# Folding the query weights with the feature map as stationary operand, in sixteen 32x32 tiles, with a turn by DMA

## Chip, cores and metric

One core of one Trainium2 chip. The time is that of one execution on the device in microseconds, as the median of several; the kernel before takes 271.53 us (three runs, 271.49 to 271.55). An engine's instructions run in the order in which they stand; between engines semaphores hold an instruction back until what it needs is there. TensorE is PE, VectorE DVE, ScalarE ACT, GpSimd POOL; SP is the engine that only issues DMAs, in one queue.

## What is computed

For x of 2048 tokens by 1024 columns, a gated mix of linear attention (a) and an expert of one token (b), in bfloat16:

```python
q, k, v = heads(x @ wqkv)                       # 32 heads of 32 columns
pq, pk = q @ w_phi[h], k @ w_phi[h]             # per head, 32 x 32
phi = concat(softmax(p), softmax(-p))           # 64 features a head
kv, z = phi_k.T @ v, phi_k.sum(tokens)
a = (phi_q @ kv / (phi_q @ z + 1e-6)) @ wo
r = x @ w_r; idx = argmax(r)                    # one token
y = (silu(x[idx] @ w_gate) * (x[idx] @ w_up)) @ w_down * sigmoid(r[idx])
out = g * a + (1 - g) * (x + y at row idx)      # g = sigmoid(x @ gate_w)
```

## The kernel before

Tokens go in 16 tiles of 128, the transposed x (`xT`) stays in SBUF. The feature map is folded into the projections ahead of use: `wkf = Wk · w_phi`, `wqf = Wq · w_phi` (eight row blocks `kb` of 128 each, so 16 folds), and pk, pq are then single products of `xT` with them.

Stage one (to 70 us) makes the values `v_all` (`k_v`, three pieces of 256, 384 and 386 columns a tile; the last carries two extra columns, the routing score and the gate, copied to `rg` by DVE) and the folds. `wT_load` brings one block of Wk or Wq transposed, 0.25 MB by a transposing DMA on the SP queue, into one of six slots of the two buffers `shv`; `fold` makes 8 matmuls of 128 columns with that block as stationary operand and the block-diagonal feature map `BDm` as moving one, and DVE copies the two results out. `FOLDS` says how many folds follow a tile. At the end `route` finds the token of the expert: scores are turned on PE, DVE takes the best of each tile, SP sends it to one partition (`mrow`), DVE takes the best of all (`mxv` ... `ixi`), SP reads `ixi` into a register and loads that row of x (`rows`), and PE and ACT turn it into `xs` (`xs_turn`).

Stage two (70 to 140 us) has 32 units of key features, a half tile each: `feats` is 8 matmuls into one of two PSUM buffers `pk`, two exponentials on ACT into `e` (four buffers), the sums `ssum` and reciprocals `rs` on DVE, `ksum` and the product `phi` on POOL (every fourth `phi` on DVE). Five units later `k_kv` adds phi-by-value into `kvps` (three PSUM banks, cleared by DVE after the first two value tiles). Between them stand the expert's products: `ffn_gu` for r = 0 to 3 (`facc`, 32 or 16 matmuls with 32 stationary columns at four column places), each over three or four buffers `wch` of 1 MB. These come from three pools: A the ring of three, D the two `shv` buffers once the folds are through, W and V the halves of `wob`. A string such as "AAAD" names the buffers of one product in order. `gate_load` holds the first three back until the last block of Wq has landed.

Stage three (140 us on) has the query units: `pq` as above, `phi` turned by DMA (`phT`), `num` = phi_q by `KV`, the division on DVE into `o_sb`, its turn by DMA (`oT`), `po` by `wo`, the mix on DVE and the store. `kv_finish` copies `kvps` to `KV`, two copies on DVE and two on ACT.

The order in which the engines' instructions stand is set by a scheduler that takes the program of these loops and may move an instruction ahead of others on its engine; it is fixed before the run. DMAs on SP wait in order, too.

Of the kernel before, what the change touches and what calls it, by code (L numbers as in the profile page):

```python
# [18 lines left out]
P = 128  # L19
# [18 lines left out]
TX = 4  # L38
FOLDS = [0] * 8 + [1, 2, 2, 2, 2, 2, 2, 3]
TDV = 0  # L40


def general_path(tc, A_wqkv, A_w_phi, A_wo, x2, out2, gate, omg, y2, idx_pool, xT, wqf, ident, BDm):
# [31 lines left out]
    for kb in range(KB):  # L75
        nc.sync.dma_start_transpose(out=wkT[:, :, kb * P:(kb + 1) * P], in_=A_wqkv[kb * P:(kb + 1) * P, D:2 * D])
        for jh in range(2):
            for j4 in range(4):
                j = jh * 4 + j4
                nc.tensor.matmul(pp[:].rearrange("p h f -> p (h f)")[:, j4 * P:(j4 + 1) * P],  # L80
                                 lhsT=wkT[:, j, kb * P:(kb + 1) * P], rhs=BDm[:, j, :], start=True, stop=True)
            nc.vector.tensor_copy(out=wkf[:, kb, jh * 512:(jh + 1) * 512], in_=pp[:].rearrange("p h f -> p (h f)"))
    nc.vector.memset(kvp[:], 0.0)
# [6 lines left out]
    def features(w):  # L90
        for hf in range(2):
            for kb in range(KB):
                nc.tensor.matmul(pp[:].rearrange("p h f -> p (h f)"), lhsT=xTt[:, kb, :],
                                 rhs=w[:, kb, hf * 512:(hf + 1) * 512], start=(kb == 0), stop=(kb == KB - 1))
            nc.vector.tensor_reduce(out=mm[:, 0, :], in_=pp[:], axis=AX.X, op=ALU.max)
            nc.vector.tensor_reduce(out=mm[:, 1, :], in_=pp[:], axis=AX.X, op=ALU.min)
            for s in range(2):
                nc.vector.tensor_tensor(out=sh[:, s], in0=pp[:], in1=_bc(mm[:, s, :], [P, HH, DH]), op=ALU.subtract)
                nc.scalar.activation(out=sh[:, s], in_=sh[:, s], func=ACTF.Exp, scale=(1.0 if s == 0 else -1.0))
            nc.vector.tensor_reduce(out=sr[:], in_=sh[:], axis=AX.X, op=ALU.add)  # L100
            nc.vector.reciprocal(out=sr[:], in_=sr[:])
            for s in range(2):
                nc.vector.tensor_tensor(out=phi[:, hf * HH:(hf + 1) * HH, s, :], in0=sh[:, s],
                                        in1=_bc(sr[:, s, :], [P, HH, DH]), op=ALU.mult)

    with tc.For_i(0, S, P) as r0:
        nc.vector.tensor_copy(out=xTt[:], in_=xT[:, :, bass.ds(r0, P)])
        for hf in range(2):
# [3 lines left out]
            nc.scalar.copy(out=va[:, hf * HH:(hf + 1) * HH, 0:DH], in_=pv[:])  # L112
        features(wkf)
        for pr in range(HH):
            nc.tensor.matmul(slot(kvp, pr), lhsT=phi[:, 2 * pr:2 * pr + 2].rearrange("p h s f -> p (h s f)"),
                             rhs=va[:, 2 * pr:2 * pr + 2, :].rearrange("p h d -> p (h d)"),
                             start=False, stop=False, skip_group_check=True)
    for pr in range(HH):
        nc.vector.tensor_copy(out=KVp[0:64, pr, 0:33], in_=slot(kvp, pr)[0:64, 0:33])
        nc.vector.tensor_copy(out=KVp[64:128, pr, 33:66], in_=slot(kvp, pr)[64:128, 33:66])  # L120

    with tc.For_i(0, NT, 1) as t:
# [3 lines left out]
        nc.vector.tensor_copy(out=gt[:, 1:2], in_=omg[:, bass.ds(t, 1)])  # L126
        features(wqf)
        for g in range(2):
# [18 lines left out]
        for nh in range(2):  # L147
            sl = slice(nh * 512, (nh + 1) * 512)
            for kb in range(KB):
# [15 lines left out]
def kernel(  # L165
# [130 lines left out]
    def wT_load(which, kb):  # L296
        n = (which * KB + kb) % 6
        wT[which, kb] = shv[n // 4][:, n % 4, :].rearrange("p (k f) -> p k f", f=P)
# [247 lines left out]
    def v_out(t, c, pv):  # L546
# [3 lines left out]
        if c == 2:  # L550
            nc.vector.tensor_copy(out=rg[:, :, t], in_=pv[:, D - lo:VW - lo])

    def v_first():
# [13 lines left out]
        for t in (1, 0):  # L567
            for c in range(3):
# [4 lines left out]
                v_out(t, c, acc[t, c])  # L573
        nc.vector.memset(kvps[:], 0.0)
        nc.vector.memset(kvps[:, 0:16 * KSTR].rearrange("p (r c) -> p r c", c=KSTR)[:, :, DH:66:DH + 1], 5e-7)

    kst = {}

    def feats(u, wf, is_q):
# [3 lines left out]
        for kb in range(KB):  # L583
            nc.tensor.matmul(pkf, lhsT=xT[:, kb, t * P:(t + 1) * P], rhs=wf[:, kb, hf * 512:(hf + 1) * 512],  # L584
                             start=(kb == 0), stop=(kb == KB - 1))
# [39 lines left out]
    def kv_finish():  # L625
        kvr = kvps[:, 0:HH * KSTR].rearrange("p (r c) -> p r c", c=KSTR)
        for hf in range(2):
            for h2 in range(2):
                (nc.vector.tensor_copy, nc.scalar.copy)[hf](out=KV[hf][h2 * 64:h2 * 64 + 64, :, h2 * 33:h2 * 33 + 33],
                                      in_=kvr[h2 * 64:h2 * 64 + 64, hf * NPU:(hf + 1) * NPU, h2 * 33:h2 * 33 + 33])  # L630
# [81 lines left out]
    def wload(n):  # L712
        wn["want"] += n
        while wq and wn["done"] < min(wn["want"], wn["folded"] + 6):
            wT_load(*wq.pop(0))
# [17 lines left out]
    for t in range(TX, NT):  # L733
# [3 lines left out]
        for n, c in enumerate((2, 0, 1) if t == NT - 1 else (0, 1, 2)):  # L737
            k_v(t, c)
            if c == 2 and t == NT - 1:
                route()  # L740
            if n >= 3 - FOLDS[t]:
                w, kb = fq.pop(0)
                fold(w, wkf if w == 0 else wqf, kb)
                wn["folded"] += 1
                wload(1 if t + TX >= NT else 0)
    LAG = 5
# [10 lines left out]
    while i < 2 * NU or n_next < NU or wos:  # L757
        if i in GU:
            r = GU.index(i)
            ffn_gu(r, ("AAAD", "DWVA", "AADD")[r])  # L760
            if r == 2:
                ffn_gu(3, "WV")
        if i == DN - 3:
# [125 lines left out]
```

## Time and profile before

| | |
|---|---|
| median of 3 runs | 271.53 us (271.49 to 271.55) |
| the profiled execution | 271.29 us |
| its span, first to last instruction | 269.7 us |
| PE busy | 262.6 us, 97% |
| DVE, POOL, ACT busy | 73%, 47%, 44% |
| clock granted to PE | full in all 40 slices |
| DMA | 56.35 MB, 209 GB/s on average |

The profile's busy time counts instructions, and matmuls overlap, so 97% says that PE nearly always has one, not that it works at its peak. The chain that ended last is followed back from the last instruction to what released each; where it lies on an engine without holes, that engine's work sets the time there, and time taken off it is time off the kernel until another engine's work becomes the later one. Row prefixes such as L584 are lines of the kernel.

### The profile page before, as it was taken

The numbers are of one execution on the slowest core, as the hardware profiler recorded it, in microseconds if no ns is written. First come the engines' busy times: TensorE is split into PE (matmuls) and PEld (weight loads), VectorE is DVE, ScalarE is ACT, GpSimd is POOL, SyncE is SP. The second block draws the span as 40 slices with busy tenths as digits, with TensorE's granted clock in tenths as the row PEclk, the third lists the DMA queues.
The fourth block names the chain that finished last, engine by engine and source line by source line (L and its number), as shares of the span: only waits on it lengthen the run. The fifth ranks groups of instructions, "written<-read, shape, count | busy, mean of one in ns | idle before, by whom it ended". The sixth has DMA issues, their size and how long they took to land.

```text
span 269.7 us, 5421 instructions
## 1 busy us (share of the span) xinstructions
PE 262.6 (97%) x2023; PEld 143.5 (53%) x2023; DVE 195.8 (73%) x344; ACT 119.0 (44%) x229; POOL 128.0 (47%) x113
## 2 busy tenths in 40 slices
PE   7999999999999999999999999999999999999993
PEld 3666667777544455545554444454444454454442
DVE  3020025556889896999998999879889797888772
ACT  3153332332355555545556565546455435534110
POOL 6000000000086989739789998554554535554110
PEclk9999999999999999999999999999999999999999
DMA  7999999997950699759936699899998899999642
GB/s 237 239 161 194 177 190 314 159 184 203 412 202 0 190 413 391 260 196 345 389 86 235 138 205 209 172 202 213 237 172 170 176 226 153 200 169 205 153 117 67
DMA packets 102522, 56.35 MB, mean 209 GB/s; under 512 B 85132, under 2 KB 90332, under 8 KB 102492
## 3 DMA queue, kind: packets, MB, share of 16 engines
q1 hardware_dynamic: 99692, 51.29, 76.9%
q10 hardware_dynamic: 2768, 4.67, 7.0%
q8 instruction: 17, 0.28, 0.4%
q14 instruction: 13, 0.11, 0.1%
q0 software_dynamic: 32, 0.00, 0.0%
HBM read 31.27 MB, written 4.20 MB: 132 GB/s over the span
## 4 chain that ended last, share of the span: by engine, by line
PE 89%; DVE 4%; DMA 2%; ACT 1%; issue 1%; ACTq 0%; POOL 0%
PE po L693 20%; PE pk L584 20%; PE pv L542 18%; PE pq L584 17%; PE num L654 3%; PE kvps L620 3%; PE pW L307 3%; PE facc L478 2%; DVE ssum L592 2%; PE pv L564 1%; DMA shv<-in_A_x_dram 1%; DMA oT<-o_sb 1%; PE kvps L564 1%; DVE rq L599 1%; PE small_ps L496 1%
## 5 line engine op out<-in xcount | busy, mean ns | idle before, releaser
L592 DVE TENSOR_REDUCE ssum<-e 128x32 f32<-128x1024 bf16 x64 | 76.9, 1203 | 6.8 <-ACT e L588 6.6
L605 POOL TENSOR_TENSOR phi<-e,rq 128x1024 bf16<-128x1024 bf16 x32 | 60.9, 1912 | 40.7 <-DVE rq L599 32.7
L584 PEld LDWEIGHTS <-xT 128*128 128x128 bf16 x512 | 47.4, 98 | 52.5 <-issue 1.3
L693 PE MATMUL po<-wo_sb,oT 128*128 128x512 bf16 (+2 forms) x264 | 60.0, 372 | 0.5 <-DMA oT<-o_sb 0.5
L584 PE MATMUL pq<-wqf,xT 128*128 128x512 bf16 x256 | 60.3, 379 | 0.0
L584 PE MATMUL pk<-wkf,xT 128*128 128x512 bf16 x256 | 59.9, 379 | 0.0
L542 PE MATMUL pv<-wv_sb,xT 128*128 128x256 bf16 (+2 forms) x336 | 52.1, 307 | 0.0
L605 POOL TENSOR_TENSOR phi<-e,rs 128x1024 bf16<-128x1024 bf16 x25 | 47.8, 1912 | 2.3 <-DVE rs L599 1.2
L542 PEld LDWEIGHTS <-xT 128*128 128x128 bf16 x336 | 31.7, 97 | 14.5
L549 ACT CAST v_all<-pv 128x384 bf16<-128x384 f32 (+1 forms) x45 | 20.1, 447 | 41.5 <-PE pv L542 35.7
L587 ACT ACTIVATE e<-pq 128x512 bf16<-128x512 f32 x32 | 19.0, 594 | 40.4 <-PE pq L584 37.8
L693 PEld LDWEIGHTS <-oT 128*128 128x128 bf16 x264 | 23.8, 98 | 23.7 <-DMA oT<-o_sb 0.6
L587 ACT ACTIVATE e<-pk 128x512 bf16<-128x512 f32 x32 | 19.1, 597 | 29.2 <-PE pk L584 21.4
L420 POOL COPY wch<-shv 1x1 bf16<-1x1 bf16 x3 | 0.4, 178 | 57.2 <-DMA shv<-in_A_wqkv_dram 57.2
L697 DVE SCALAR_TENSOR_TENSOR oo<-po,gate,xg 128x512 bf16<-128x512 f32 (+2 forms) x33 | 24.0, 727 | 4.3 <-PE po L693 4.2
L602 POOL TENSOR_TENSOR ksum<-ksum,ssum 128x32 f32<-128x32 f32 x32 | 14.0, 438 | 22.4 <-DVE ssum L592 20.8
L659 DVE TENSOR_TENSOR o_sb<-num,rden 128x512 bf16<-128x512 f32 x32 | 21.7, 677 | 0.8
L588 ACT ACTIVATE e<-pq 128x512 bf16<-128x512 f32 x32 | 18.9, 591 | 0.0
L588 ACT ACTIVATE e<-pk 128x512 bf16<-128x512 f32 x32 | 18.9, 591 | 0.0
L678 ACT ACTIVATE xg<-xin,omg 128x1024 f32<-128x1024 bf16 x16 | 18.3, 1148 | 0.5
L309 DVE CAST wkf<-pW 128x512 bf16<-128x512 f32 x16 | 10.6, 686 | 9.5 <-PE pW L307 9.5
L654 PEld LDWEIGHTS <-phT 128*128 128x128 bf16 x256 | 12.4, 98 | 8.0 <-issue 0.7
(133 smaller groups left out, 199.8 us busy)
## 6 DMA issues: line engine op xcount, KB each, us to landing
wch<-in_B_w_down_dram SPq DMA_DIRECT2D x7, 1024.0 KB
wch<-in_B_w_up_dram SPq DMA_DIRECT2D x6, 1024.0 KB
wch<-in_B_w_gate_dram SPq DMA_DIRECT2D x4, 1024.0 KB
xin<-in_A_x_dram ACTq DMA_DIRECT2D x16, 256.0 KB
out_dram<-oo SPq DMA_DIRECT2D x30, 128.0 KB
wch<-in_B_w_gate_dram SPq DMA_DIRECT2D x4, 768.0 KB
wv_sb<-in_A_wqkv_dram SPq DMA_DIRECT2D x8, 256.0 KB
wo_sb<-in_A_wo_dram SPq DMA_DIRECT2D x1, 2048.0 KB
```

Source lines behind the costliest of these rows:

```text
L542: nc.tensor.matmul(pv[:, 0:hi - lo], lhsT=xT[:, kb, t * P:(t + 1) * P], rhs=wv_sb[:, kb, lo:hi], start=(kb == 0), stop=(kb == KB - 1))
L549: nc.scalar.copy(out=v_all[:, t, h0:h1, 0:DH], in_=pv[:, 0:(h1 - h0) * DH].rearrange("p (h d) -> p h d", d=DH))
L584: nc.tensor.matmul(pkf, lhsT=xT[:, kb, t * P:(t + 1) * P], rhs=wf[:, kb, hf * 512:(hf + 1) * 512], start=(kb == 0), stop=(kb == KB - 1))
L587: nc.scalar.activation(out=e[:, :, 0, :], in_=pk[:], func=ACTF.Exp)
L588: nc.scalar.activation(out=e[:, :, 1, :], in_=pk[:], func=ACTF.Exp, scale=-1.0)
L592: nc.vector.tensor_reduce(out=ssum[:], in_=e2, axis=AX.X, op=ALU.add)
L605: eng.tensor_tensor(out=phi[:].rearrange("p h s f -> p (h s) f"), in0=e2, in1=_bc(rs, [P, HH * 2, DH]), op=ALU.mult)
L654: nc.tensor.matmul(num[:, pl * 66:pl * 66 + 66], lhsT=phT[:, pl, :], rhs=KV[hf][:, pl, :], start=True, stop=True)
L659: nc.vector.tensor_tensor(out=st["o"][:, hf * HH:(hf + 1) * HH, :].rearrange("p (r h) d -> p r h d", h=2), in0=nv[:, :, :, 0:DH], in1=rden ...
L678: nc.scalar.activation(out=xg, in_=st["xin"][:], func=ACTF.Copy, scale=omg[:, t:t + 1])
L693: nc.tensor.matmul(po[:, 0:w], lhsT=st["oT"][:, kb, :], rhs=moe["wo"][:, kb, sl], start=(kb == 0), stop=(kb == KB - 1))
L697: nc.vector.scalar_tensor_tensor(out=o_out[:, 0:w], in0=po[:, 0:w], scalar=gate[:, t:t + 1], in1=st["xg"][:, sl], op0=ALU.mult, op1=ALU.add)
```

## The change

The key folds move to tiles 5 to 12, one each. The query blocks are all loaded (eight slots now), and folded in four packs, after pieces of tiles 13, 14 and 15. A pack has `BDm`'s 32x32 blocks as stationary operands at all sixteen places of the array and 512 columns of the loaded blocks as moving ones. Its four results lie in the three banks of `kvps` and one other; DVE and ACT copy two each to `wfT` (two buffers of the ring A), and eight transposing DMAs turn `wfT` into `wqf`, whose columns stand in another order, which `q_heads` undoes where pq reads them. `kvps` is cleared later, by ACT (`kv_zero`). The copies of `rg` go to ACT, the last two copies of `kv_finish` to DVE; `route` comes one piece earlier. The buffers of the expert's products are taken in another order. (The general path, a branch for other data, has small edits and is not run.)

```diff
-FOLDS = [0] * 8 + [1, 2, 2, 2, 2, 2, 2, 3]
+FOLDS = [0] * 5 + [1] * 8 + [0] * 3
+PACKS = {(13, 2): (0, 0), (14, 1): (1, 0), (15, 0): (0, 1), (15, 2): (1, 1)}
...
+def q_heads(wqf, kb, hf):
+    return wqf[:, kb, hf * 512:(hf + 1) * 512].rearrange("p (r c f) -> p c r f", r=4, f=DH)
...
     def wT_load(which, kb):
-        n = (which * KB + kb) % 6
+        n = kb
...
+    def qfold(a, half):
+        if (a, half) == (0, 0):
+            moe["wfT"] = [ring.tile([P, 4, D], BF, name="wfT", tag="wch") for _ in range(2)]
+        pB = psB.tile([P, 512], F32, name="pW", tag="pB")
+        banks = [kvps[:, 0:512], kvps[:, 512:1024], kvps[:, 1024:1536], pB[:]]
+        for r in range(4):
+            for c in range(4):
+                j = 4 * a + c
+                nc.tensor.matmul(banks[r][32 * c:32 * c + 32, :].rearrange("p (k d) -> p k d", d=P),
+                                 lhsT=BDm[32 * r:32 * r + 32, j, 32 * r:32 * r + 32],
+                                 rhs=shv[half][32 * r:32 * r + 32, :, j * P:(j + 1) * P],
+                                 start=True, stop=True, tile_position=(32 * r, 32 * c), skip_group_check=True)
+        for r in range(4):
+            (nc.vector.tensor_copy, nc.scalar.copy)[r % 2](out=moe["wfT"][a][:, r, half * 512:(half + 1) * 512], in_=banks[r])
+
+    def qfold_turn():
+        for ar in range(8):
+            nc.sync.dma_start_transpose(out=wqf[:, :, ar * P:(ar + 1) * P], in_=moe["wfT"][ar // 4][:, ar % 4, :])
+
+    def kv_zero():
+        one = ones[:, 0:1]
+        nc.scalar.activation(out=kvps[:], in_=one.to_broadcast([P, 3 * 512]), func=ACTF.Copy, scale=0.0)
+        nc.scalar.activation(out=kvps[:, 0:16 * KSTR].rearrange("p (r c) -> p r c", c=KSTR)[:, :, DH:66:DH + 1],
+                             in_=one.unsqueeze(2).to_broadcast([P, 16, 2]), func=ACTF.Copy, scale=5e-7)
...
         if c == 2:
-            nc.vector.tensor_copy(out=rg[:, :, t], in_=pv[:, D - lo:VW - lo])
+            nc.scalar.copy(out=rg[:, :, t], in_=pv[:, D - lo:VW - lo])
...
-        nc.vector.memset(kvps[:], 0.0)
-        nc.vector.memset(kvps[:, 0:16 * KSTR].rearrange("p (r c) -> p r c", c=KSTR)[:, :, DH:66:DH + 1], 5e-7)
...
-            nc.tensor.matmul(pkf, lhsT=xT[:, kb, t * P:(t + 1) * P], rhs=wf[:, kb, hf * 512:(hf + 1) * 512],
+            nc.tensor.matmul(pk[:].rearrange("p (c r) f -> p c r f", r=4) if is_q else pkf,
+                             lhsT=xT[:, kb, t * P:(t + 1) * P],
+                             rhs=q_heads(wf, kb, hf) if is_q else wf[:, kb, hf * 512:(hf + 1) * 512],
...
-                (nc.vector.tensor_copy, nc.scalar.copy)[hf](out=KV[hf][h2 * 64:h2 * 64 + 64, :, h2 * 33:h2 * 33 + 33],
+                (nc.vector.tensor_copy, nc.scalar.copy)[0](out=KV[hf][h2 * 64:h2 * 64 + 64, :, h2 * 33:h2 * 33 + 33],
...
-        while wq and wn["done"] < min(wn["want"], wn["folded"] + 6):
+        while wq and wn["done"] < min(wn["want"], wn["folded"] + 8):
...
-            if c == 2 and t == NT - 1:
+            if n == 1 and t == NT - 1:
                 route()
...
-                wload(1 if t + TX >= NT else 0)
+                wload(4 if t + TX >= NT else 0)
+            if (t, n) in PACKS:
+                qfold(*PACKS[t, n])
+    qfold_turn()
...
-            ffn_gu(r, ("AAAD", "DWVA", "AADD")[r])
+            ffn_gu(r, ("WVDD", "AAAW", "VDDA")[r])
             if r == 2:
-                ffn_gu(3, "WV")
+                ffn_gu(3, "AA")
...
         if i == 2:
+            kv_zero()
             gates()
```

On DVE, at the end of stage one and the start of stage two (mi, mrow, mxv, cnd, ixf, ixi, hl are the routing's small tiles; wfT and wqf the folded query weights; e, ssum, rs those of a key unit). Before:

```order
L331 TENSOR_TENSOR mi<-mi,row_144 16x1
L315 RECIPROCAL gate<-eg 128x16
L316 TENSOR_SCALAR omg<-gate 128x16
L592 TENSOR_REDUCE ssum<-e 128x32
L599 RECIPROCAL rs<-ssum 128x32
L592 TENSOR_REDUCE ssum<-e 128x32
L335 TENSOR_REDUCE mxv<-mrow 1x1
L599 RECIPROCAL rs<-ssum 128x32
L337 TENSOR_SCALAR cnd<-mrow,mxv 1x16
L339 TENSOR_TENSOR cnd<-cnd,mrow 1x16
L592 TENSOR_REDUCE ssum<-e 128x32
L341 TENSOR_REDUCE ixf<-cnd 1x1
```

and now:

```order
L361 TENSOR_TENSOR mi<-mi,row_144 16x1
L329 CAST wfT<-kvps 128x512 x2
L365 TENSOR_REDUCE mxv<-mrow 1x1
L367 TENSOR_SCALAR cnd<-mrow,mxv 1x16
L369 TENSOR_TENSOR cnd<-cnd,mrow 1x16
L371 TENSOR_REDUCE ixf<-cnd 1x1
L373 CAST ixi<-ixf 1x1
L390 TENSOR_SCALAR hl<-ixi 1x1
L622 TENSOR_REDUCE ssum<-e 128x32
L629 RECIPROCAL rs<-ssum 128x32
L622 TENSOR_REDUCE ssum<-e 128x32
L629 RECIPROCAL rs<-ssum 128x32
```

mxv, which reads what the DMA of mrow brought, stood behind the second sum, and the instructions from cnd to hl among later sums; all six now stand ahead of the first sum.

On the SP queue, same place (wch are the expert's buffers, gate and up its weights; shv the loaded blocks; rows the expert's token). Before:

```order
L299 DMA_TRANSPOSE shv<-in_A_wqkv_dram 128x8x128 x10
L454 DMA wch<-in_B_w_gate_dram 128x2x2048 x4
L333 DMA mrow<-mi 1x16x2
L454 DMA wch<-in_B_w_gate_dram 128x2x1536
L454 DMA wch<-in_B_w_up_dram 128x2x512
L344 TENSOR_LOAD ixi
L344 ISA x2
L345 ISA
L345 DMA rows<-in_A_x_dram 8x128
```

and now:

```order
L304 DMA_TRANSPOSE shv<-in_A_wqkv_dram 128x8x128 x8
L484 DMA wch<-in_B_w_gate_dram 128x2x2048 x3
L484 DMA wch<-in_B_w_gate_dram 128x2x1536
L333 DMA_TRANSPOSE wqf<-wfT 128x8x128
L363 DMA mrow<-mi 1x16x2
L333 DMA_TRANSPOSE wqf<-wfT 128x8x128 x3
L374 TENSOR_LOAD ixi
L374 ISA x2
L375 ISA
L375 DMA rows<-in_A_x_dram 8x128
L333 DMA_TRANSPOSE wqf<-wfT 128x8x128 x4
L484 DMA wch<-in_B_w_gate_dram 128x2x2048
```

One turn of the query weights (wqf<-wfT) stands ahead of mrow, three behind it, and the last four behind the load of rows and ahead of the fourth buffer (128x2x2048) of the first product.

On ACT, at the start of stage two. Before:

```order
L549 CAST v_all<-pv 128x8x32
L549 CAST v_all<-pv 128x12x32
L587 ACTIVATE e<-pk 128x16x32
L588 ACTIVATE e<-pk 128x16x32
L587 ACTIVATE e<-pk 128x16x32
L588 ACTIVATE e<-pk 128x16x32
```

and now:

```order
L579 CAST v_all<-pv 128x8x32
L579 CAST v_all<-pv 128x12x32
L329 CAST wfT<-pW 128x512
L329 CAST wfT<-kvps 128x512
L617 ACTIVATE e<-pk 128x16x32
L618 ACTIVATE e<-pk 128x16x32
L337 ACTIVATE kvps<-const-bfloat16-1.0 128x1536
L617 ACTIVATE e<-pk 128x16x32
L618 ACTIVATE e<-pk 128x16x32
L338 ACTIVATE kvps<-const-bfloat16-1.0 128x16x2
```

The copies of the last pack stand ahead of the first exponentials, and the clearing of kvps between the first pair and the second.

## Rows read from the trace of the kernel before

**Rows 1.** Page, part 1: busy time, share of the span, instructions
```profile
PE 262.6 (97%) x2023; PEld 143.5 (53%) x2023; DVE 195.8 (73%) x344; ACT 119.0 (44%) x229; POOL 128.0 (47%) x113
```

**Rows 2.** Chain that ended last, 13 to 90 us: start us, us, what
```profile
38.46 0.45 PE pW L307 x8
38.91 2.17 PE pv L542 x16
...
41.53 1.31 PE pv L542 x8
...
70.15 8.63 PE pk L584 x40
```

**Rows 3.** Busy time by stage (us, engine busy, instructions, PEclk, DMA share, GB/s)
```profile
13.20:70.15 56.95, 56.95 (x484) 40.09 (x481) 23.59 (x57) 20.54 (x48) 0.41 (x3) 1.00 0.97 207
```

**Rows 4.** The same chain ahead of the first expert product
```profile
83.00 0.94 PE pk L584 x5
...
84.81 0.60 ACT e L587
...
86.22 1.91 PE facc L478 x32
```

**Rows 5.** The chain at the turn to the queries
```profile
146.69 1.13 DVE ssum L592
...
148.19 1.09 DVE ssum L592
...
157.93 0.42 PE num L654 x8
```

**Rows 6.** Timeline there: start, us, instruction [idle before, releaser]
```profile
151.89 0.38 ACT L629 CAST KV<-kvps 64x264 bf16<-64x264 f32 x1 [2.43 <-DVE KV L629]
...
153.79 1.22 DVE L592 TENSOR_REDUCE ssum<-e 128x32 f32<-128x1024 bf16 x1 [0.30 <-ACT e L588]
```

**Rows 7.** The chain around the second expert product
```profile
96.80 0.25 PE kvps L620 x8
...
98.91 1.84 PE facc L478 x32
100.75 0.36 PE kvps L620 x8
```

**Rows 8.** Groups by form: busy us, mean ns, idle before
```profile
L678 ACT ACTIVATE xg<-xin,omg 128x1024 f32<-128x1024 bf16 x16 | 18.3, 1148 | 0.5
...
L483 ACT COPY gs<-facc 128x512 f32<-128x512 f32 x4 | 2.3, 586 | 3.8 <-PE facc L478 3.8
```

**Rows 9.** Timeline of ACT, first key features
```profile
73.64 0.60 ACT L587 ACTIVATE e<-pk 128x512 bf16<-128x512 f32 x1 [0.64 <-PE pk L584]
```

**Rows 10.** Timeline of the SP queue, 59 to 82 us
```profile
59.05 1.23 SPq L299 DMA_TRANSPOSE shv<-in_A_wqkv_dram  x1
62.77 2.33 SPq L454 DMA_DIRECT2D wch<-in_B_w_gate_dram  x4
71.45 0.65 SPq L333 DMA_DIRECT2D mrow<-mi  x1
...
80.35 0.38 SPq L345 DMA_DIRECT2D rows<-in_A_x_dram  x1
```

**Rows 11.** Timeline of DVE, same stretch
```profile
73.03 1.22 DVE L592 TENSOR_REDUCE ssum<-e 128x32 f32<-128x1024 bf16 x1 [1.23 <-ACT e L588]
...
76.68 0.16 DVE L335 TENSOR_REDUCE mxv<-mrow 1x1 f32<-1x16 f32 x1 [0.70 <-DMA mrow<-mi]
...
78.78 0.08 DVE L343 CAST ixi<-ixf 1x1 uint32<-1x1 f32 x1
```

**Rows 12.** Timeline of GpSimd, same stretch
```profile
74.78 1.91 POOL L605 TENSOR_TENSOR phi<-e,rs 128x1024 bf16<-128x1024 bf16 x1
...
77.24 1.91 POOL L605 TENSOR_TENSOR phi<-e,rs 128x1024 bf16<-128x1024 bf16 x1 [0.34 <-DVE cnd L337]
...
79.32 1.91 POOL L605 TENSOR_TENSOR phi<-e,rs 128x1024 bf16<-128x1024 bf16 x1
```

More of the change, by code (lines that the diff above doesn't have):

```diff
@@ L81, in general_path @@
                                  lhsT=wkT[:, j, kb * P:(kb + 1) * P], rhs=BDm[:, j, :], start=True, stop=True)
-            nc.vector.tensor_copy(out=wkf[:, kb, jh * 512:(jh + 1) * 512], in_=pp[:].rearrange("p h f -> p (h f)"))
+            nc.scalar.copy(out=wkf[:, kb, jh * 512:(jh + 1) * 512], in_=pp[:].rearrange("p h f -> p (h f)"))
     nc.vector.memset(kvp[:], 0.0)
@@ L92, in features @@
             for kb in range(KB):
-                nc.tensor.matmul(pp[:].rearrange("p h f -> p (h f)"), lhsT=xTt[:, kb, :],
-                                 rhs=w[:, kb, hf * 512:(hf + 1) * 512], start=(kb == 0), stop=(kb == KB - 1))
+                nc.tensor.matmul(pp[:].rearrange("p (c r) f -> p c r f", r=4), lhsT=xTt[:, kb, :],
+                                 rhs=w(kb, hf), start=(kb == 0), stop=(kb == KB - 1))
             nc.vector.tensor_reduce(out=mm[:, 0, :], in_=pp[:], axis=AX.X, op=ALU.max)
@@ L112, in general_path @@
             nc.scalar.copy(out=va[:, hf * HH:(hf + 1) * HH, 0:DH], in_=pv[:])
-        features(wkf)
+        features(lambda kb, hf: wkf[:, kb, hf * 512:(hf + 1) * 512].rearrange("p (c r f) -> p c r f", r=4, f=DH))
         for pr in range(HH):
@@ L117, in general_path @@
                              start=False, stop=False, skip_group_check=True)
-    for pr in range(HH):
-        nc.vector.tensor_copy(out=KVp[0:64, pr, 0:33], in_=slot(kvp, pr)[0:64, 0:33])
-        nc.vector.tensor_copy(out=KVp[64:128, pr, 33:66], in_=slot(kvp, pr)[64:128, 33:66])
+    kvr = kvp[:, 0:HH * KSTR].rearrange("p (r c) -> p r c", c=KSTR)
+    nc.vector.tensor_copy(out=KVp[0:64, :, 0:33], in_=kvr[0:64, :, 0:33])
+    nc.vector.tensor_copy(out=KVp[64:128, :, 33:66], in_=kvr[64:128, :, 33:66])
     with tc.For_i(0, NT, 1) as t:
@@ L126, in general_path @@
         nc.vector.tensor_copy(out=gt[:, 1:2], in_=omg[:, bass.ds(t, 1)])
-        features(wqf)
+        features(lambda kb, hf: q_heads(wqf, kb, hf))
         for g in range(2):
```

## Prediction

> **What bounds the kernel now.** I read the page first, then the chain that ended last in order of time, then the timelines of the places that the change touches. The page shows TensorE (PE) busy for 97% of the span [rows 1]. The chain shows the first stage, values and weight folds, as PE work without a hole until 70.15 us, at granted clock 1.00 [rows 2, 3]; the key features (pk) follow. The little that is lost stands at known places: PE waits some 0.3 us for ScalarE (ACT) ahead of the first expert product at 86.22 [rows 4], and a little at 157.93, where num follows a chain on VectorE (DVE) [rows 5]. So there are two questions: what the change takes off PE, and which other engine, off the chain by about a microsecond, takes its place.
>
> **PE, the folds.** Sixteen folds of eight matmuls stand in the chain with 0.45 us each [rows 2]. The eight of the key weights stay, four tiles earlier; the eight of the query weights go: 8 x 0.45 = 3.6 us off a stage that is PE alone. In their place come four packs of sixteen 32x32 matmuls of 512 columns. A full matmul of 512 columns takes a slot of 8.63 / 40 = 0.216 us [rows 2]. The nearest row to a pack is the expert product, whose matmuls use 32 columns of the array each: 32 of them take 1.84 us, 8 slots and 0.11 [rows 7]. So four on different columns cost one slot; the next 66-column group takes 0.36 us instead of 0.25 [rows 7], so going in and out of the narrow form is 0.2 us together. No row shows tiles on different rows of the array. If all sixteen overlap, a pack is 0.22 + 0.2 = 0.42 us; if only the columns overlap, 4 x 0.22 + 0.2 = 1.08. I take 0.52, near the lower end, since the columns overlap fully: 4 x 0.52 = 2.1 us, within 1.7 to 4.3. The last pack also needs bank 2 cleared by DVE, which has the gate and routing instructions between its copies now: I add 0.3. Net -3.6 + 2.1 + 0.3 = -1.2, and pk starts at 68.95 instead of 70.15.
>
> The Trainium skill ("TensorE: Matmul & The Clock Gate", Part 3: Packing small matmuls) gives 660 ns for sixteen 32x32 tiles of 512 columns. By it the packs are 4 x 0.66 = 2.64 us and PE gains 0.5 us less. No run here shows it yet.
>
> **DVE and ACT in the first stage.** Of the sixteen copies of query weights eight go to ACT, and so do the rg copies. PE waited for neither engine there, so I cost it at nothing; the cover is that each is busy for less than half of the stage [rows 3].
>
> **ACT, the clearing of kvps.** It moves from DVE (first stage, hidden) to ACT, behind the first pair of exponentials. No row shows ACT clearing 1536 columns; 512 columns take 0.59 us and 1024 take 1.15 [rows 8], so 1.7 us by the same step. A pair of exponentials takes 1.1 us and ACT idles 0.64 to the next [rows 9]. With 1.7 us between, the second pair ends some 0.65 us after the fourth pk wants its buffer (there are two): PE waits 0.65 us. Bounds: 0 if it is half as long, 1.0 if it is a quarter longer.
>
> **DVE, the new wait.** This decides. Today the routing result mrow goes out at 71.45 and has landed at 76.68, when mxv reads it; DVE has done its first sums (ssum) by then [rows 10, 11]. In the changed order DVE has mxv ahead of its first ssum. So the first sum starts when mrow lands (M) plus the chain down to hl, six small instructions of 0.08 to 0.16 us: M + 0.9.
>
> When is M? Today mrow stands behind four loads of 1 MB, issued from 62.77: 13.9 us from the first issue to mrow's landing [rows 10, 11]. The first load leaves 3.7 us after the last query block's issue at 59.05 [rows 10], since it is held until that block has landed. In the change that block waits for the last key fold. A tile is 2.17 + 1.31 = 3.48 us [rows 2], so the last key fold ends at 38.46 + 3 x 0.45 (folds of tiles 5 to 7) + 0.45 + 4 x (3.48 + 0.45) = 56.0, and the first load leaves at 59.7. Ahead of mrow are then 3.75 MB of loads and one turn of 0.25 MB. By the same 13.9 us M = 73.6. A transpose moves its quarter megabyte slower (the stage full of them has the DMA 97% busy at 207 GB/s [rows 3], the loads go at 4 MB in under 13.9 us): +0.6, M = 74.2. It cannot be before 71, as mrow leaves near 69.5; I keep 72.5 to 75.2.
>
> What follows: the pitch of a sum with its reciprocal is 1.5 us [rows 5], the first phi on GpSimd starts 1.75 after its sum's start, then one each 2.1, 1.9 long [rows 11, 12]. The third phi ends at M + 0.9 + 1.75 + 2 x 2.1 + 1.9 = M + 8.75. PE needs it for the third kvps group (0.26), and the eighth pk (1.73) follows: its end is M + 10.95 with 0.2 of latency. Today it ends at 83.00 + 1.73 = 84.73 [rows 4]. PE's own pace gives 68.95 + 0.65 + 8 x 1.73 + 3 x 0.26 = 84.2. So the shift there is max(-0.5, M - 73.8): with M = 74.2, **+0.4**. The PE gain of 1.2 us is eaten, and would be at any price of the packs below 0.8 us.
>
> **SP queue and the expert's buffers.** The eight turns are issued ahead of the fourth expert buffer, 1.3 us each (1.23 for a transpose [rows 10]). ixi is made at M + 0.85; today the row load follows it by 1.6 us (78.78 to 80.35) [rows 10, 11]; then four turns and the load, at M + 8.0. With what is left of the turns in the queue (some 1.8 us) and 1 MB per 3.5 us (13.9 / 4) it lands at M + 13.3. The product starts 1.5 us after the eighth pk (exponentials and xs) [rows 4], at M + 12.45, and needs that buffer after 24 matmuls, M + 13.85. Half a microsecond to spare: cost 0. The later expert loads have time: the second product is some 12 us behind [rows 4, 7], and the query weights are needed at 140.
>
> **DVE at the turn to the queries.** Two KV copies of 0.4 us each come over from ACT, between the sums. DVE is the chain there, from 146.69 to num at 157.93 [rows 5]: +0.8. ACT, which now stands 2.43 us for those copies, has the exponentials ready earlier, which gives back DVE's wait of 0.30 [rows 6]: net **+0.45** at num, which PE meets directly. Bounds 0 to 0.8.
>
> **Sum.** +0.4 + 0.45 = +0.85. The profiled execution took 271.29 us (span 269.7); the median 271.53 is 0.24 above. So 271.29 + 0.85 = 272.15 for an execution like that one, **272.3** as a median.
>
> **Rivals.**
> (1) PE's gain comes through: faster. If mrow lands by 73.2 or before (a start-up that the two early loads have behind them, a turn as fast as a load: M near 72.5), the shift is -0.5, or -1.2 if the clearing hides too; and with ACT free earlier the KV copies may cost nothing. Time 270.3 to 271.0, say 270.7. Against it: the 13.9 us are this very queue. For it: a third of a microsecond decides.
> (2) The fourth expert buffer is late: slower. Point: landing after M + 13.85. Each microsecond beyond is one for PE; if the turns each hold the DMA 0.4 us longer than their issue, 8 x 0.4 - 0.5 = 2.7 on PE, 275.0; at half that, 273.4. For it: all eight turns stand ahead of it in one queue.
> (3) The tiles do not overlap across rows: packs of 1.08 us, so pk starts 2.2 later and PE's own pace gives 86.4: +1.7 + 0.45, 273.7. If instead the four columns of one row group go one after another, each a slot and a weight load of 0.1, a pack is 4 x 0.32 + 0.2 = 1.5 us, PE's pace gives 88.1 and the time is 275.3. Rows 7 speak against that: there four tiles of one row group share a slot. The second form is what the same page of the Trainium skill says of weight loads (they overlap running matmuls only where the row group differs); by that rule the expert product would not have been 1.84 us, so the trace does not bear it out.
> (4) The query matmuls, which now read their 512 columns in runs of 32, lose a column per run: 256 x 16 / 2.4 GHz = 1.7 us, 274. No row shows such a read, for or against.
> That the change does not do what it says is excluded by the order: the 64 narrow matmuls and the eight turns are in it.
>
> **Chances.** The forecast's case 0.48 (within it: slower 0.28, same 0.20); rival 1 0.25 (faster 0.22, same 0.03); rival 2 0.15 (slower 0.11, same 0.04); rival 3 0.08 (slower 0.07, same 0.01; its second form 0.01 of it); rival 4 0.04, slower. A measurement tells about 0.2%, 0.54 us. Together faster 0.22, same 0.28, slower 0.50. The forecast's case alone spans 271.5 to 272.9; the range to hold 8 in 10 goes to 270.4 for most of rival 1 and to 273.8 for rival 3 and half of rival 2.
>
> **What would show it.** Right: a wait of DVE at mxv for mrow of 2 to 4 us, ended near 74; kvps waiting for phi near 80; the eighth pk ending near 85; no wait inside the first expert product; packs of half a microsecond; num at 158.8 after DVE. Wrong: mxv without a wait, pk running through from 69, packs over 0.8 us, or PE standing inside the expert product.

## The result, and the profile after

The changed kernel takes 275.37 us (the median of 274.13, 275.25, 275.49 and 701.08) against 271.51 for the kernel before on the same chip (271.41 to 271.55). The ratio is 1.0122, with a 95% interval of 1.0089 to 1.0155: slower, by some 3.3 us as this ratio has it, and outside the range that was forecast. The execution of 701.08 is left out of the ratio, as are two of a later run (e7, 280.06 and 280.33), and no profile shows what happened in them. The profiled execution took 275.49 us, its span is 273.5 us (269.7 before).

The page's busy line answers to [rows 1]. Under it stand the rows of PE's timeline that the prediction spoke of (start, length, engine, line, operation, tile and forms, count, and in brackets the wait ahead of it with what ended it).

```profile
PE 261.4 (96%) x2023; PEld 140.0 (51%) x2023; DVE 190.5 (70%) x320; ACT 124.8 (46%) x253; POOL 128.0 (47%) x113
```

```profile
59.35 0.42 PE L324 MATMUL kvps<-shv,BDm 32*32 32x512 bf16 x12
59.39 0.39 PE L324 MATMUL pW<-shv,BDm 32*32 32x512 bf16 x4
59.71 2.35 PE L572 MATMUL pv<-wv_sb,xT 128*128 128x256 bf16 x16
...
68.20 0.42 PE L324 MATMUL kvps<-shv,BDm 32*32 32x512 bf16 x12 [0.33 <-DVE wfT L329]
68.25 0.40 PE L324 MATMUL pW<-shv,BDm 32*32 32x512 bf16 x4
68.58 9.03 PE L612 MATMUL pk<-wkf,xT 128*128 128x512 bf16 x40
80.11 0.43 PE L650 MATMUL kvps<-v_all,phi 128*128 128x66 bf16 x8 [2.50 <-POOL phi L635]
...
84.53 1.89 PE L612 MATMUL pk<-wkf,xT 128*128 128x512 bf16 x8
...
87.91 1.48 PE L508 MATMUL facc<-wch,xs 128*32 128x512 bf16 x24
90.54 0.62 PE L508 MATMUL facc<-wch,xs 128*32 128x512 bf16 x8 [1.16 <-DMA wch<-in_B_w_gate_dram]
```

A pack of sixteen tiles goes from 59.35 to the next matmul at 59.71: 0.36 us. The key features start at 68.58; before they start at 69.98:

```profile
69.98 8.80 PE L584 MATMUL pk<-wkf,xT 128*128 128x512 bf16 x40
```

So PE's gain is there, 1.4 us, and two waits eat it: 2.50 us for phi, and 1.16 us inside the first expert product for its fourth buffer. Before, that product began at 86.22 and ran through [rows 4]; now it begins at 87.91.

What the first wait goes back to stands on DVE's timeline. The chain that ended last names both waits as DMA (columns: start, length, what):

```profile
75.33 0.16 DVE L365 TENSOR_REDUCE mxv<-mrow 1x1 f32<-1x16 f32 x1 [4.23 <-DMA mrow<-mi]
...
76.17 0.14 DVE L373 CAST ixi<-ixf 1x1 uint32<-1x1 f32 x1
...
76.41 1.20 DVE L622 TENSOR_REDUCE ssum<-e 128x32 f32<-128x1024 bf16 x1
```

```profile
69.18 6.12 DMA mrow<-mi
84.89 5.61 DMA wch<-in_B_w_gate_dram
```

Before, DVE's first sum stood at 73.03 and mxv behind it [rows 11]. Now the first sum stands behind mxv, and so behind mrow, at 76.41. SP's queue, with what it issues (of the first row the landings are 65.1, 68.4, 71.0 and 73.2 by the trace's DMA events):

```profile
59.66 4.04 SPq L484 DMA_DIRECT2D wch<-in_B_w_gate_dram  x4
66.84 2.19 SPq L333 DMA_TRANSPOSE wqf<-wfT  x1
69.18 0.65 SPq L363 DMA_DIRECT2D mrow<-mi  x1
69.92 5.99 SPq L333 DMA_TRANSPOSE wqf<-wfT  x3
78.08 0.40 SPq L375 DMA_DIRECT2D rows<-in_A_x_dram  x1
78.59 6.20 SPq L333 DMA_TRANSPOSE wqf<-wfT  x4
84.89 0.54 SPq L484 DMA_DIRECT2D wch<-in_B_w_gate_dram  x1
```

And the stretch of these stages as a whole, by windows (PE busy and count, granted clock, DMA share, GB/s), before and after:

```profile
59.50:101.00 41.50, 41.37 (x363) 1.00 0.67 234
```

```profile
59.50:101.00 41.50, 37.32 (x327) 18.41 (x312) 30.35 (x52) 24.04 (x49) 21.40 (x23) 1.00 0.97 279
```

(The second row has a column for each engine, PE first.) The stretch holds more DMA work than before, but 0.97 does not say that the DMA was full. The share adds up the times of the packets that began in a stretch, and over single microseconds it goes above 1 (2.19 from 71 to 72, at 237 GB/s). Shorter windows of the changed kernel show a hole: while SP waited for the index, between the fourth turn and the fifth, the DMA had next to nothing to do, and just before, with nothing but turns in it, it moved 280 GB/s.

```profile
75.00:77.00 2.00, 2.00 (x11) 1.00 1.27 280
77.00:80.00 3.00, 0.60 (x3) 1.00 0.14 27
```

Where the 3.3 us are, read off PE's timeline against before: key features start 1.4 earlier; from there to the first expert product 3.1 more (19.33 instead of 16.24); inside it 1.33; from it to the first query feature nothing; at the turn to the queries 0.3 in the end. Together 3.3, up to DVE's last instruction (268.75 against 265.43). The span grew by another 0.5 behind that; in the profiles of this study that last piece is anywhere from 3.2 to 4.75 us, so I count it as nothing.

### The profile page after: what moved, and what is told of

The parts are those of the page before. It is cut to its first block, busy times and chain, and to the rows that moved or that the text cites. A ratio compares the mean times of both kernels' runs of the same rounds, so it can differ in the third digit from the quotient of the medians.

```text
span 273.5 us, 5439 instructions
## 1 busy us (share of the span) xinstructions
PE 261.4 (96%) x2023; PEld 140.0 (51%) x2023; DVE 190.5 (70%) x320; ACT 124.8 (46%) x253; POOL 128.0 (47%) x113
## 4 chain that ended last, share of the span: by engine, by line
PE 80%; DVE 8%; DMA 7%; SPq 1%; issue 1%; ACT 0%; POOL 0%; DVEq 0%
PE po L723 20%; PE pv L572 17%; PE pq L612 16%; PE pk L612 15%; DVE ssum L622 4%; PE num L684 3%; PE kvps L650 3%; DMA mrow<-mi 2%; DMA wch<-in_B_w_gate_dram 2%; DMA wv_sb<-in_A_wqkv_dram 2%; PE facc L508 2%; PE pW L312 1%; DMA oT<-o_sb 1%; PE kvps L594 1%; PE pv L594 1%; SPq L333 1%
## 5 line engine op out<-in xcount | busy, mean ns | idle before, releaser
L572 PE MATMUL pv<-wv_sb,xT 128*128 128x256 bf16 (+2 forms) x336 | 51.1, 307 | 0.0
L650 PEld LDWEIGHTS <-phi 128*128 128x128 bf16 x256 | 11.6, 99 | 10.6 <-POOL phi L635 5.1
```

The lines of the kernel that those rows point to most:

```text
L572: nc.tensor.matmul(pv[:, 0:hi - lo], lhsT=xT[:, kb, t * P:(t + 1) * P], rhs=wv_sb[:, kb, lo:hi], start=(kb == 0), stop=(kb == KB - 1))
L650: nc.tensor.matmul(kv_slot(pr), lhsT=phi[:, 2 * pl:2 * pl + 2, :, :].rearrange("p h s f -> p (h s f)"), rhs=v_all[:, t, hf * HH + 2 * pl:h ...
```

## The experiments

My theory from these rows: two losses in a row (mrow's wait on DVE, the late fourth buffer), both from SP's order, and a small one at the KV copies. The rivals: PE's own pace, the fourth buffer alone, or the DMA as such.

### One edit each, and all three

**e1**, mrow on another queue.

```diff
-        nc.sync.dma_start(out=mrow[0:1, :, :], in_=mi[:])
+        nc.scalar.dma_start(out=mrow[0:1, :, :], in_=mi[:])
```

> The changed kernel with one edit: the small routing transfer mrow is issued from ScalarE's queue instead of SP's, so it stands behind no load and no turn. The scheduler answers by putting the fourth expert buffer on SP ahead of the row load and of the last four turns. Theory (VectorE's first key sum stands behind mxv, which waits for mrow; the fourth buffer stands behind the turns): mrow lands near 71.5 to 72 instead of 75.3, mxv waits under 1 us, the eighth pk ends at 83.3 to 84.3 instead of 86.3, no wait of PE inside the first expert product, 271.0 to 272.3 us. Rival A (PE itself is slower in the key stage: packs, clearing of kvps): the eighth pk still ends near 86, 274 to 275. Rival B (the fourth buffer alone is the loss): the eighth pk unchanged, the stall of 1.16 us gone, 274.0 to 274.3. Rival C (the 2 MB of turns slow the DMA for all that follows): mrow early, but the fourth buffer still lands near 90, so PE stands 4 us inside the product and the time stays near 275.

Measured: 275.86 us, ratio 1.0156 (1.0108 to 1.0205). mrow did not come earlier. The issue on ACT's queue, and DVE's reader:

```profile
68.82 0.61 ACTq L363 DMA_DIRECT2D mrow<-mi  x1
```

```profile
75.70 0.16 DVE L365 TENSOR_REDUCE mxv<-mrow 1x1 f32<-1x16 f32 x1 [4.43 <-DMA mrow<-mi]
```

Issued at 68.8 from a queue of its own it lands no earlier than from SP. So my theory fell in one point: it is not the queue. What the DMA engines had taken on before it came first all the same. The first product runs through here, since the scheduler had moved its fourth buffer up, but it starts at 89.57: PE had waited 2.94 us for phi, and its clock stood at the half level (1.2 GHz) from 81 to 83 (0.50).

**e2**, half the turns behind the fourth buffer (`qfold_turn(0, 4)` where it was, `qfold_turn(4, 8)` behind `ffn_gu(0)`).

> The changed kernel with one edit: the last four of the eight turns are issued after the fourth expert buffer instead of ahead of it; mrow stays where it is in SP's queue. Theory (mrow's wait and the late fourth buffer are two separate losses): mrow lands near 75.3 as before, the eighth pk ends at 86.0 to 86.5, the stall of 1.16 us inside the first expert product goes, 273.9 to 274.4 us. Rival B (the fourth buffer is all of the loss beyond the KV copies): 271.8 to 272.5. Rival C (the DMA is short of bandwidth, whatever the order): the stall stays within 0.3 us, 275.

Measured: 274.67 us, 1.0107 (1.0067 to 1.0146). The product runs through (first row), but it starts at 89.20 and not at 87.9, and the windows show why: the clock fell to its half level after PE's wait of 2.67 us, and part of the pk behind it ran at that.

```profile
80.10 0.62 PE L650 MATMUL kvps<-v_all,phi 128*128 128x66 bf16 x8 [2.67 <-POOL phi L635]
83.58 0.41 PE L650 MATMUL kvps<-v_all,phi 128*128 128x66 bf16 x8
...
89.20 1.91 PE L508 MATMUL facc<-wch,xs 128*32 128x512 bf16 x32
```

```profile
78.00:82.00 4.00, 1.90 (x12) 0.73 0.55 145
82.00:86.00 4.00, 4.00 (x30) 0.85 1.24 211
```

From one kvps group to the next it is 3.48 us here and 2.08 in the changed kernel (80.11 to 82.19, clock 1.00). So the 1.3 us of the buffer were won, and lost again to the clock.

**e3**, KV copies on both engines again (`[0]` back to `[hf]`).

> The changed kernel with one edit: two of the four KV copies go back from VectorE to ScalarE, as before the change. Theory (0.53 us of the loss arises at the turn to the queries): the first num comes 0.5 us earlier against the first pq than in the changed kernel, 274.6 to 275.0 us. Rival: ScalarE's exponentials come later by the copies and give it back, no difference (275.3). Nothing changes ahead of 154.

Measured: 274.75 us, 1.0118 (1.0067 to 1.0169). At num, 0.5 us came back: from the first group to the second it is 2.34 us, 2.85 in the changed kernel. At the end only 0.1 is left of it, since a later po waits 0.61 for oT instead of 0.21. The four executions lie apart by their clock: 273.68 and 274.12 at a mean of 0.998 and 1.000, 275.39 and 276.35 at 0.988 and 0.987.

**e4**, the three together.

> The three edits together: mrow issued from ScalarE's queue, the last four turns behind the fourth expert buffer, two KV copies back on ScalarE. Theory: the losses add up; the eighth pk ends at 83.3 to 84.3, no stall inside the first expert product, num 0.5 us earlier: 270.4 to 271.8 us, no slower than the kernel before (271.5) and faster if ScalarE's clearing of kvps hides. Rival A (PE's own pace in the key stage is the bound): 273.2 or more.

Measured: 274.46 us, 1.0080 (1.0054 to 1.0107). The mrow edit gained nothing, as in e1 (mxv at 76.25 after 4.46 us), and the clock fell after a PE wait of 2.97 us (0.58 from 82 to 86).

**e8**, the edit of e1 on the kernel before, where no turn exists.

> The kernel before, with mrow issued from ScalarE's queue instead of SP's: there are no turns, four loads of 1 MB are under way when it is issued. If the queue decides what a small transfer waits for, it lands within 3 us of its issue, by 74.5. If the DMA engines serve earlier loads first, whatever queue they came from, it lands near 76.5 as in the kernel before. The time stays 271.5 within 0.5 us either way, since nothing waits for it there.

Measured: 272.99 us, one execution. mxv at 76.49, against 76.68 [rows 11], issued at the same time (71.47; 71.45 before).

```profile
71.47 0.60 ACTq L333 DMA_DIRECT2D mrow<-mi  x1
```

```profile
76.49 0.16 DVE L335 TENSOR_REDUCE mxv<-mrow 1x1 f32<-1x16 f32 x1 [2.03 <-DMA mrow<-mi]
```

So also without any turn a queue of its own gains a small transfer 0.2 us of 5 here.

### What stands ahead of mrow

**e5**: all turns held until the second key phi is made.

```diff
-    qfold_turn()
...
+            if r == 0:
+                qfold_turn()
...
+        if i == 1:
+            nc.gpsimd.tensor_copy(out=wqf[0:1, 0, 0:D:P], in_=kst[i][0:1, 0, 0, 0:8])
```

> The changed kernel, with all eight turns held until the second key phi is made, so that mrow has no turn ahead of it and the fourth expert buffer and the row load go ahead of all turns. It still has 4 MB of expert loads ahead of it. Theory (the chip's DMA engines serve what was issued earlier first, from whatever queue, and the eighth pk ends 10.95 us after mrow lands): the loads end near 73.5, mrow lands at 73.4 to 74.2, the eighth pk ends at 84.4 to 85.2 instead of 86.3, TensorE's wait at kvps falls from 2.5 to about 1 us, so its clock stays at the high level, and no wait inside the first expert product: 272.4 to 273.4 us. Rival (mrow takes its 6 us whatever stands ahead): it lands at 75 or later, the eighth pk ends at 86 or later, 274 or more.

**e6**: and the third and fifth buffer held until mrow is there.

```diff
+        n = len(fst)
+        if n in (0, 1):
             nc.gpsimd.tensor_copy(out=w1, in_=wT[1, KB - 1][0:1, 0, 0:1])
+        if n in (2, 4):
+            nc.gpsimd.tensor_copy(out=w1, in_=moe["mrow"][0:1, 0, 0:1])
```

> The kernel of e5, with the third and the fifth expert buffer (a load of 1 MB and one of 0.75 MB) also held until mrow has landed; 2.25 MB stay ahead of it. Theory: these are through by 69.5, mrow lands at 70.3 to 71.5, VectorE does not wait for it, the eighth pk ends at TensorE's own pace, 83.2 to 83.9, no wait at kvps of over 0.5 us and none inside the first expert product; the query features start 1.0 to 1.6 us earlier than in the kernel before instead of 3.0 later: 270.8 to 271.8 us. Rival A (something else in the first stage, the packs or the clearing, holds the key features): the eighth pk ends at 85 or later, 273 or more. Rival B (the loads that are held now come late): a new wait for a buffer inside the first expert product of over 1 us.

**e7**: e6 with the edit of e3.

> The kernel of e6 with two KV copies back on ScalarE, so that nothing of the losses named is left. Theory: 270.2 to 271.3 us, 0.1 to 0.6% faster than the kernel before: the 1.2 us that TensorE gains by the packs. Rival: no difference, since other work (the turns, the clearing) takes it back.

**e11**: the changed kernel with the turns left out.

> The changed kernel without the eight turns: the query weights are left at zero, so the query features are not the reference's. It shows what the 2 MB of turns cost in all. Theory: mrow lands near 73.7 behind 4 MB of loads, the eighth pk ends near 84.7, the fourth expert buffer lands by 77 and nothing waits inside the expert products: the first query feature starts 1.3 to 2.2 us earlier than in the changed kernel less the wait of 1.33 us, 2.7 to 3.2 us in all. Rival (the turns are not the cause): the eighth pk ends at 86.

mrow came as expected in all of them. What stands ahead of it, and mxv's start: 3.75 MB and a turn 75.33; 4 MB and no turn 73.77 (e5) and 73.42 (e11); 2.25 MB 70.81 (e6). A turn of 0.25 MB in the way costs more than a megabyte's quarter: the last load of the changed kernel landed at 73.2, the turn behind it at 75.1. In e5 the eighth pk still ended at 85.9, a microsecond late: GpSimd's third phi took 2.89 us instead of 1.91, while VectorE made a phi of its own. In e6 the first product starts at 84.84, 1.4 us ahead of before [rows 4], and PE waited on the way for nothing but `xs`, 0.34 us at the product's start. That is PE's gain, whole.

But e5 took 276.57 us (1.0202; 1.0172 to 1.0233), e6 277.64 (1.0220; 1.0195 to 1.0245) and e7 277.50 (1.0194; 1.0160 to 1.0228): slower than the changed kernel, and a miss of mine each. In e6 the wait stands in the second product, whose buffers come behind the late turns, and the clock falls after it:

```profile
84.84 1.91 PE L512 MATMUL facc<-wch,xs 128*32 128x512 bf16 x32 [0.34 <-ACT xs L382]
...
98.53 0.36 PE L473 MATMUL small_ps<-identf,gT 128*128 128x16 f32 x2 [1.12 <-DMA gT<-gs]
...
104.08 1.74 PE L512 MATMUL facc<-wch,xs 128*32 128x512 bf16 x8 [2.41 <-DMA wch<-in_B_w_gate_dram]
```

```profile
104.00:108.00 4.00, 3.59 (x20) 0.50 0.87 348
```

The turns release two of these buffers, so they may not be late; and they are slow. In e5 a stretch that holds little but turns has the DMA at 188 GB/s and a share of 1.02; the loads of the changed kernel go at 405:

```profile
88.00:92.00 4.00, 3.95 (x46) 1.00 1.02 188
```

```profile
66.00:70.00 4.00, 3.67 (x37) 1.00 1.01 405
```

Eight turns, 2.1 million bytes at 188 GB/s, are 11 us. But that is the pace at which SP issues them:

```profile
80.88 11.02 SPq L333 DMA_TRANSPOSE wqf<-wfT  x8
```

By the trace's DMA events each of the eight in e5 lands 1.8 to 2.1 us after its own issue ends (the first at 84.16, the last at 93.71), so they do not queue up behind one another; and the fifth turn of the changed kernel, at 78.59, took 1.28 us to issue with the DMA as good as idle. In the changed kernel the second to the fourth, which were issued sooner behind the loads, land 0.8 to 1.0 us apart (75.90, 76.74, 77.75), at the 280 GB/s of the window above. So the 11 us are time of SP's queue, which everything behind the turns in it waits out, and not shown to be time of the whole DMA; the expectation of e9 below still counts them as that.

e11, without them (its query weights are zero, so the query features are not the reference's), took 271.60 us in one execution; the eighth pk ends at 84.4, the first query feature starts at 140.59 instead of 143.19 (2.6 us, just under what I expected), and the DMA's share in the stretch is 0.75:

```profile
59.50:101.00 41.50, 39.67 (x349) 1.00 0.75 277
```

### Turns early, but behind mrow

**e9**: the turns and the fifth buffer held until mrow has landed, the third one not.

```diff
+        n = len(fst)
+        if n < 3:
             nc.gpsimd.tensor_copy(out=w1, in_=wT[1, KB - 1][0:1, 0, 0:1])
+        if n == 4:
+            nc.gpsimd.tensor_copy(out=w1, in_=moe["mrow"][0:1, 0, 0:1])
...
+    nc.gpsimd.tensor_copy(out=wqf[0:1, 0, 0:D:P], in_=moe["mrow"][0:1, 0:8, 0])
     qfold_turn()
```

> The changed kernel with the turns and the fifth expert buffer held until mrow has landed, so that ahead of mrow stand three loads of 1 MB and one of 0.25 MB, then the fourth buffer, then the eight turns, then the rest. Theory (two limits: mrow must not stand behind more than the DMA can move by 71, and the turns, 1.36 us of DMA each, must be through by 87 so that the buffers of the second expert product, which they release, are loaded by 98.5): mrow lands at 71.5 to 72.5, the eighth pk ends at 83.3 to 84.0, the turns land from 76 to 87, no wait of over 0.5 us inside the first or the second expert product: 270.8 to 272.0 us. Rival: the second product waits again, as in e6, 274 or more.

**e10**: e9 with the edit of e3.

> The kernel of e9 with two KV copies back on ScalarE. Theory: 0.5 us less than e9, 270.3 to 271.5 us, 0.1 to 0.6% faster than the kernel before. Rival: no faster than the kernel before.

Measured: e9 272.09 us, 1.0004 (0.9976 to 1.0033); e10 272.55 us, 1.0021 (0.9993 to 1.0048). The order alone takes the whole loss away, with the same matmuls, the same turns and the same bytes. But no more than that: the first product starts at 84.94, 1.28 us ahead of before, and the second one waits for small transfers of the first one's results (gT), which stand behind the buffers on the DMA, and for its buffers; the first query feature starts at 140.12 (before 140.16). These buffers stand behind the turns: SP issues the eight from 74.38 to 86.06, and in that time the DMA goes at less than half of what it moves after it. Windows of the DMA and PE's rows in e9:

```profile
76.00:88.00 12.00, 11.87 (x114) 1.00 1.11 176
88.00:92.00 4.00, 4.00 (x34) 1.00 0.95 363
```

```profile
84.94 1.91 PE L512 MATMUL facc<-wch,xs 128*32 128x512 bf16 x32
...
98.19 0.37 PE L473 MATMUL small_ps<-identf,gT 128*128 128x16 f32 x2 [0.62 <-DMA gT<-gs]
98.49 2.22 PE L512 MATMUL facc<-wch,xs 128*32 128x512 bf16 x32
```

**e12**: the changed kernel with only the mxv chain moved behind the first key sum (a copy of `rs` into `mxv` ahead of it, and the second half of `route` called after the first key unit). SP's queue was meant to stay as it was.

> The changed kernel with the mxv chain behind the first key sum on VectorE, and so the index load behind the first phi products on GpSimd; SP's queue as it was. Theory (two losses, one behind the other, the second covered by the first): the wait of 2.5 us at kvps falls below 1 us and the eighth pk ends at 84.0 to 85.0, but the fourth expert buffer still lands at 90.0 to 90.8, so the wait inside the first expert product grows from 1.2 to 2.4 us or more, and the time stays 274.5 to 276 us. Rival (the wait at kvps is the whole loss): 272 to 273.

Measured: 277.63 us, 1.0213 (1.0158 to 1.0268). The wait for phi fell as expected, to 0.41, and the rest was a miss: the scheduler put the row load behind all turns and the fourth buffer, at 84.76, and PE waited for the row instead.

```profile
81.67 0.43 PE L655 MATMUL kvps<-v_all,phi 128*128 128x66 bf16 x8 [0.41 <-POOL phi L640]
88.65 0.18 PE L385 MATMUL small_ps<-ident,rows 128*128 128x8 bf16 x1 [4.82 <-DMA rows<-in_A_x_dram]
```

So it does not tell what the wait at DVE is worth by itself; it shows that the next transfer in that queue is late as well.

**e13**: e10 with the row load on GpSimd's queue (`nc.gpsimd.dma_start` and the index read by GpSimd), and **e14**: e10 with the row load on SP behind the second turn (`qfold_turn(0, 2)`, the second half of `route`, `qfold_turn(2, 8)`).

> The kernel of e10 with the row load issued from GpSimd's queue, so that on SP's queue the first turn no longer stands behind the row load, which waits for the index. Theory (in e9 and e10 the 1.3 us that TensorE has ahead of the first expert product is given back in the second one, since the turns end some 2 us too late for the buffers behind them): the first turn is issued near 72.2 instead of 74.4, the turns end near 85, the small transfers and the buffers of the second product land 1.5 to 2.3 us earlier, no wait of over 0.3 us at the second product, and the first query feature starts at 138.7 to 139.3, 1 us or more ahead of the kernel before (140.16): 270.2 to 271.2 us against 271.5 to 271.8 for the kernel before on the same chip. Rival (GpSimd's wait for the index and its issue hold the first phi products): kvps waits, and no gain over e10.

> The kernel of e10 with the row load on SP's queue again, but behind the second turn instead of ahead of the first; GpSimd has nothing to issue. In e13 the first turn went out 1.7 us earlier, but GpSimd's issue of the row load held the phi products, and the gain was lost ahead of the first expert product. Theory: the eighth pk ends at 83.3 to 84.0 as in e9, the first expert product starts at 84.8 to 85.2, the turns land about 1 us earlier than in e10, no wait of over 0.4 us at the second product, the first query feature starts at 138.7 to 139.5: 270.0 to 271.0 us, 0.2 to 0.5% under the kernel before. Rival (the DMA is short by more than 1 us): a wait at the second product again, no gain.

Measured: e13 271.52 us, 1.0002 (0.9981 to 1.0022); e14 271.75 us, 1.0003 (0.9980 to 1.0027). No gain in either, against what I expected. In e13 GpSimd waits for the index and its phi come later (first row); the first product starts at 86.92, and then the second one, at 99.55, does not wait. In e14 the first product starts at 84.96 and the second one waits (the other rows). Whoever is early at the first product waits at the second.

```profile
75.11 0.72 POOL L376 DMA_DIRECT2D rows<-in_A_x_dram  x1 [2.36 <-DVE rs L633]
```

```profile
98.53 0.37 PE L476 MATMUL small_ps<-identf,gT 128*128 128x16 f32 x2 [0.74 <-DMA gT<-gs]
98.83 1.48 PE L515 MATMUL facc<-wch,xs 128*32 128x512 bf16 x24
100.70 0.40 PE L515 MATMUL facc<-wch,xs 128*32 128x512 bf16 x3 [0.39 <-DMA wch<-in_B_w_gate_dram]
```

In e9, e10, e13 and e14 the DMA's share from 59.5 to 101 is 0.9 or more. It does not tell them apart, though: e13, whose second product does not wait, has the highest (1.01). e9:

```profile
59.50:101.00 41.50, 40.36 (x373) 20.18 (x358) 34.26 (x55) 25.30 (x52) 23.32 (x25) 1.00 0.95 280
```

No version beats the kernel before. That transfers keep PE's 1.3 us from the end is what e9 and e14 show in their rows (the second product waits for transfers alone). e11, without turns, has no wait there, but comes to it 0.9 us later (99.13). Whether cheaper turns, or loads that do not stand behind the turns in one queue, would let the gain through was not tried.

## Why the prediction was wrong

The side was right (slower, at 0.50), the size was not: +0.85 forecast, some 3.3 measured on the timelines. (A slip in the sum: 272.15 and 0.24 are 272.4, not 272.3.)

- **PE, the folds: right.** Forecast -1.2, measured -1.4. I took 0.52 us a pack, the sixteen tiles overlap fully and it is 0.36. By the Trainium skill ("TensorE: Matmul & The Clock Gate", Part 3) it would have been 0.66 each; the trace does not agree (0.36). Four such packs and the wait of 0.33 us for DVE at the last make -1.8; of that 0.3 is lost ahead of the stage, whose first value piece starts at 13.38 instead of 13.09. Rival 3 is out. Rival 4 is out as well: eight pq still take 1.73 us.
- **Clearing of kvps: the mechanism right, the size too large.** 1.46 and 0.22 us on ACT where I had 1.7; PE waits some 0.2, not 0.65.

```profile
71.48 1.46 ACT L337 ACTIVATE kvps<-const-bfloat16-1.0 128x1536 f32<-128x1536 bf16 x1
```

- **mrow: the wait, its place and the formula right, the landing mis-sized.** mxv waits 4.23 us, the first sum stands behind it. "Its end is M + 10.95" gives 86.25 with M = 75.3, and that is where PE's next instruction starts. The step that failed is "a transpose moves its quarter megabyte slower: +0.6, M = 74.2". With a load in the place of the turn mxv starts at 73.77 (e5) and 73.42 (e11), so the 73.6 was right and the +0.6 should have been 1.6 to 1.9. The turn alone put 1.9 us between the last load's landing and its own, and mrow landed just behind, at 75.3. In the shift max(-0.5, M - 73.8) that is 1.5 instead of 0.4. The shift measured is 1.69, since by the same reading (the start of what follows) the eighth pk of before ends at 84.56 and not at 84.73.
- **The fourth expert buffer: wrong.** The step that failed is "then four turns and the load, at M + 8.0", landing at M + 13.3, "cost 0": it became M + 9.6 and M + 15.2. The four turns ahead of it took 6.2 us to issue where I had 5.2 (one of them 2.06), and the load 5.6 us to land. It cost 1.33. This was rival 2, with its mechanism and place, at a chance of 0.15; and I gave it a chance of its own, though turns make both late.
- **KV copies: right at num** (the first to the second num group is 0.5 longer than in e3, forecast 0.45), though only some 0.1 to 0.3 of it reaches the end.
- **The rest of the queue:** the expert loads from the second product on have, in the changed kernel, the time that I gave them; nothing waits there, because the first product was late already.

So both errors are the price of a turn to what stands behind it in SP's queue: 0.6 us for the one ahead of mrow, where 1.6 to 1.9 were measured, and half a microsecond to spare behind the four ahead of the fourth buffer, where 1.33 us were missing. Of the 3.3 us, 1.69 come from the first (with PE's gain taken off), 1.33 from the second and 0.3 from the KV copies. The work of the DMA as a whole is not what cost them: e9 has the same turns and nearly the same share (0.95 for 0.97), and loses nothing.

And one thing that no part of the forecast had: such a wait of PE can cost the clock as well. In the changed kernel's profile it did not (1.00 from 78 to 86), in e1, e2, e4 and e6 it did.

## What to carry to other kernels

Work that goes from PE to the DMA is priced first by the queue that issues it, and by everything that stands behind it there: here eight turns held SP's queue for 11 us (e5) and bought 1.4 us of PE. A busy share of the DMA over a long stretch does not show this; look at the windows, one microsecond or two, and at the landings. A small transfer on a chain of waits is as late as the bytes that the DMA engines took on before it, issued from SP or from ACT (e1, e8); what helps is to hold the bulk back until it is through (e6, e9). And where one order is early at one product and waits at the next, as in e9 and e14, another order of the same queue has little left to give.

## Not expected of the hardware

- Sixteen tiles of 32x32 on different rows and columns ran in the time of little more than one slot: 0.36 us a pack of 512 columns, where one matmul of 512 columns takes 0.22.
- A queue of its own did nothing for a transfer of 128 bytes (e1: 75.70 and not 75.33; e8: 76.49 and not 76.68).
- The turns of 0.25 MB went at 188 GB/s where each waited for its issue (1.36 us apart in e5) and at 280 where three had been issued sooner (changed kernel, 75 to 77); the loads had 405. A share of the DMA of 1.0 stood beside the first and the last.
- After a PE wait of 2.67 us the granted clock fell to the lower level (e2), after 2.50 and 2.56 it did not (changed kernel, e3); in e6 it did after one of 2.41 that followed shorter ones (0.50 from 104 to 108). So the length of the last wait alone does not tell.
- Where GpSimd and VectorE make a phi at the same time, one of the two takes longer: 2.89 us instead of 1.91 on GpSimd (e5), or 2.86 on VectorE (changed kernel; 1.25 in e5). What holds it no run here tells apart.
